# Reordering the first steps of a fused causal convolution and swish MLP: taps by DMA, bf16 blocks, output matmuls later

## The chip, the cores and the metric

The kernel runs on one core of a Trainium2 chip, in one launch. The metric is device time in microseconds (us). The core has a matrix engine (PE, or TensorE, with its weight loads PEld), a vector engine (DVE), a scalar engine (ACT, or ScalarE), GpSimd (POOL) and a sync engine (SP) that here only issues DMAs. POOL and ACT issue DMAs too. Each engine works through its own instructions in order and waits on semaphores for the others; DMAs run beside them all. Matmuls write to PSUM, from where DVE or ACT take the results to SBUF.

## The reference

Two things follow each other. The first is a causal depthwise convolution over the sequence with 7 taps; the taps are a softmax per head, 8 heads of 24 channels each. The second is an MLP with a swish whose slope `beta` differs per hidden channel.

```
x: (8, 4096, 192) f32;  weight: (8, 7);  w_in: (192, 2048);  w_out: (2048, 192);  beta: (2048,)
w   = softmax(weight, axis=-1)                      # 8 heads, 7 taps
y   = for each token: sum over k of w[head, k] * x[token - 6 + k]     (zeros before the sequence)
h   = y.reshape(32768, 192) @ w_in
g   = h * sigmoid(beta * h)
out = g @ w_out                                     # (32768, 192) f32
```

The kernel uses g*beta = silu(beta*h): ACT computes silu with `beta` as scale, and w_out is divided by beta beforehand.

## The kernel before, in words

**Streams and steps.** The 32768 tokens are two streams of 16384 (`NS = 2`) that go side by side. The 192 channels lie as three groups (`NK = 3`) of 64, so one stream fills 64 partitions and two fill 128. `steps` lists the chunks of each stream: step 0 and 1 of 128 tokens, step 2 to 8 of 256, the rest of 512. A tile is 512 tokens, a block 128, so steps 0 to 2 cover tile 0 with blocks 0, 1 and 2 to 3.

**What a step does.** For each of 16 groups of 128 hidden channels (`fc`) PE computes w_in times the convolved input into PSUM (`ph`, two buffers), and ACT takes it through silu into `g` (bf16, SBUF). In steps 0 to 2 `mm1_pair` (matmuls on line 315, ACT on line 319) does two groups at once, `u` and `u + 8`: the lower partitions use one half of w_in, the upper ones the other, so that w_in need be loaded only once by then. From step 3 on `mm1` (lines 332, 336) does one group for both streams, with the copies of w_in that `copy_w_in` (116) makes in the other partitions. The output matmuls of step i, `mm2` (366), read `g` and w_out_s and run during step i+1: `mm2_plan` spreads them over its units. They come in two phases, since PE works with 64 rows at a time on two banks; phase 1 ends with `store`, where DVE takes out the two banks (372) and SP stores them. In steps of 512 `mm2_quarters` (412) takes this place.

**The convolution.** From step 3 on DVE does it: 7 operations (296, 298) per step on transposed input `xt`, in the order of a work list that `vector_work` empties by a budget of DVE time. Tile 0 is convolved on PE instead: `transpose_0` (206) turns a block of `x0` with an identity matrix, `take_0` (211 on ACT, 213 on DVE) copies it to `xr[b]`, `halo_0` (217) copies its last 6 columns to the front of the next block's `xr`, `conv_0` (223) multiplies it by diagonal matrices `diag` of the taps, summing over the taps in PSUM, and `evac_0` (232, 234) scales by 1/sum and writes `xcp`. For tile 1, blocks 0 and 1 are transposed on PE too (540), the later ones by DMA transposes on SP (97) after a cast on DVE (86).

**The start.** The 8x7 taps are loaded by SP; a matmul with a selection matrix `sel` (made by POOL, 146) spreads them over 128 partitions (183); DVE takes the maximum (185), ACT the exponential (188). `warm` matmuls (178) on a tile of zeros keep PE busy before. POOL's queue then issues, in this order: w_in in pieces (113), blocks 2 and 3 of x (129) among them, w_out (157), tile 1 of x (80) and, after a wait, the copies of w_in. `scale_w_out` (268) divides w_out by beta on DVE, four groups at a time.

**Order.** Almost all instructions are pinned to program order, so each engine does them as the code lists them: in steps 0 and 1 the `if` chains in the main loop put transposes, convolution matmuls and scalings between the pairs of the first layer.

Of the kernel before, what the change touches and what calls it, by code (L numbers as in the profile page):

```python
# [19 lines left out]
def kernel(  # L20
# [17 lines left out]
    NK = 3  # L38
# [20 lines left out]
    g_pool = ctx.enter_context(tc.tile_pool(name="g", bufs=1))  # L59
# [59 lines left out]
    taps = consts.tile([H, K], FP32, name="taps")  # L119
    pin(nc.sync.dma_start(out=taps, in_=weight))  # L120
    x0 = consts.tile([128, NB, NS, D], FP32, name="x0")
    pin(nc.scalar.dma_start(out=x0[:, 0, 1, :], in_=xs[1, 0:128, :]))
    pin(nc.sync.dma_start(out=x0[:, 0, 0, :], in_=xs[0, 0:128, :]))
# [4 lines left out]
    def load_x0(b, eng):  # L128
        pin(eng.dma_start(out=x0[:, b, :, :],
                          in_=xs[:, 128 * b:128 * b + 128, :].rearrange("s p d -> p s d")))  # L130
# [3 lines left out]
    zeros = consts.tile([128, 256], BF16, name="zeros")  # L134
    pin(nc.vector.memset(zeros, 0.0))
# [5 lines left out]

    sel = consts.tile([H, NS, H, Q // H], FP32, name="sel")
    pin(nc.vector.memset(sel, 0.0))
    ident = consts.tile([128, 128], FP32, name="ident")
    pin(nc.vector.memset(ident, 0.0))
    pin(nc.gpsimd.affine_select(out=sel, in_=sel, compare_op=ALU.not_equal, fill=1.0, base=0,  # L146
                                pattern=[[0, NS], [-1, H], [0, Q // H]], channel_multiplier=1))
# [10 lines left out]
    for b in (0, 2):  # L158
        for s in range(NS):
            load_x(1, s, b, b + 2, nc.gpsimd)  # L160


    xr = [consts.tile([128, NK, PAD + 128], FP32R, name=f"xr{b}") for b in range(NB)]
    pin(nc.vector.memset(xr[0][:, :, 0:PAD].bitcast(FP32), 0.0))
# [8 lines left out]

    idle = psum_h.tile([128, 2, TILE], FP32, name="ph")

    def warm(n, cols):
        for _ in range(n):
            pin(nc.tensor.matmul(idle[:, 0, 0:cols], zeros[:, 0:128], zeros[:, 0:cols], start=True, stop=True))

    warm(8, 256)  # L180
    cv0 = psum_h.tile([128, 2, TILE], FP32, name="ph")
    tap_ps = cv0[:, 1, 0:K]
    pin(nc.tensor.matmul(tap_ps, sel.rearrange("h s g j -> h (s g j)"), taps, start=True, stop=True))
    nmax = consts.tile([128, 1], FP32, name="nmax")
    pin(nc.vector.tensor_reduce(out=nmax, in_=tap_ps, axis=AX.X, op=ALU.max, negate=True))
    etap = consts.tile([128, K], FP32, name="etap")
    tsum = consts.tile([128, 1], FP32, name="tsum")
    pin(nc.scalar.activation(etap, tap_ps, AF.Exp, bias=nmax, accum_out=tsum))
# [13 lines left out]
    def transpose_0(bank, b, src=x0):  # L202
        t = bank[:, 0:NK * 128].rearrange("p (k t) -> p k t", k=NK)
        v = src[:, b, :, :].rearrange("p s d -> p (s d)").rearrange("p (m k) -> p k m", k=NK)
        for kk in range(NK):
            pin(nc.tensor.transpose(t[:, kk, :], v[:, kk, :], ident))  # L206
        return t

    def take_0(t, b, act=False):
        if act:  # L210
            pin(nc.scalar.activation(xr[b][:, :, PAD:], t, AF.Copy))
        else:
            pin(nc.vector.tensor_copy(xr[b][:, :, PAD:], t))

    def halo_0(t, b):
        dst = xr[b + 1][:, :, 0:PAD] if b + 1 < NB else xt_of[0][:, :, TILE + LEAD - PAD:]
        pin(nc.vector.tensor_copy(dst, t[:, :, 128 - PAD:]))

    def conv_0(cv, b, k0=0, k1=K):

        for k in range(k0, k1):
            for s in range(NS):
                pin(nc.tensor.matmul(  # L223
                    cv[s][:, 0:NK * 128], diag[half_of(s), k, :, :].rearrange("p s q -> p (s q)"),
                    xr[b][half_of(s), :, k:k + 128], start=(k == 0), stop=(k == K - 1)))
# [12 lines left out]
    t = transpose_0(pa[0], 0)  # L238
    take_0(t, 0, act=True)
    warm(4, 128)  # L240
# [4 lines left out]
    halo_0(t, 0)  # L245
# [4 lines left out]
    pb = po_banks()  # L250
# [4 lines left out]
    beta_ps = idle[:, 1, 0:NF]  # L255
# [3 lines left out]
    t = transpose_0(pa[0], 1)  # L259
    take_0(t, 1)  # L260
    halo_0(t, 1)
# [46 lines left out]
    def mm1_pair(i, u):  # L308
# [9 lines left out]
        for h in range(2):  # L318
            pin(nc.scalar.activation(g_of[i][:, fcs[h], :, 0:n],  # L319
# [3 lines left out]
    def mm1(i, fc):  # L323
# [12 lines left out]
        pin(nc.scalar.activation(g_of[i][:, fc, :, 0:n], ph[:, :, 0:n], AF.Silu,  # L336
                                 scale=beta[:, fc:fc + 1]))

    def pairs_of(i):
        if steps[i][1] == 128:  # L340
            return [((0, 0), (1, 0))]
        return [((s, 0), (s, 1)) for s in range(NS)]

    def mm2_plan(i):
# [3 lines left out]
        if len(prs) == 1:  # L348
            order = [(prs[0], 0, 2 - 2 * i, 6), (prs[0], 1, 10, 16)]
        else:  # L350
            order = [(prs[p], ph, 8 * ph + 4 * p, 8 * ph + 4 * p + 4) for ph in range(2) for p in range(2)]
# [6 lines left out]
    def mm2(i, pr, phase, fc):  # L358
        if phase == 0 and fc == 0:
            po_of[pr] = po_banks()  # L360
        po = po_of[pr]
        for half in range(2):
# [3 lines left out]
            pin(nc.tensor.matmul(po[q][:, 0:D], g_of[i][r, fc, s, ts(b, 128)], w_out_s[r, fc, :],  # L366
# [33 lines left out]
    def mm2_quarters(count):  # L400
        for _ in range(count):
            turn = turns.pop(0)
            for s in range(NS):
                for r in range(2):
# [3 lines left out]
                    if (i, m) not in po_of:  # L408
# [4 lines left out]
                                         g_of[i][half_of(r), fc, s, 0:n],  # L413
# [28 lines left out]
    def last(i):  # L442
# [3 lines left out]
        for s in range(NS):  # L446
            for b in range(n // 128):
                po = po_bank()
                for fc in range(NF):
                    pin(nc.tensor.matmul(po[:, 0:D], g_of[i][:, fc, s, ts(b, 128)], w_out_s[:, fc, :],  # L450
# [35 lines left out]
    gs = [g_pool.tile([128, NF, NS, TILE], BF16, name=f"g{p}") for p in range(2)]  # L486
    for i in range(n_steps):
        plan = mm2_plan(i - 1) if 0 < i <= NQ else [[] for _ in range(NF)]
        g_of[i] = gs[i % 2]
        if i == 0:  # L490
            cv1, cv2, cv3 = pb, pa, pb
            for u in range(NF // 2):
                mm1_pair(0, u)
                if u == 0:
                    t = transpose_0(pb[0], 2)
                    take_0(t, 2)
                    halo_0(t, 2)
                elif u == 1:
# [96 lines left out]
```

## Time and profile before

| what | value |
|---|---|
| median of 9 runs | 692.16 us (691.69 to 694.86) |
| the profiled execution's own time | 691.73 us |
| its span, first to last instruction | 690.0 us |
| PE / ACT / DVE / POOL busy | 99% / 85% / 80% / 2% of the span |
| step 0 starts on PE (line 315) | 8.33 us |
| step 3 starts on PE (line 332) | 34.06 us |

The profile is one execution, taken by the hardware. Times count from the span's start. A group of instructions has its busy time and the idle time just before it, with what ended that idle time (the releaser). A busy PE is not PE at its peak, since matmuls are pipelined and their ends are modelled. Idle time on an engine that does not set the pace costs nothing.

### The profile page before, as it was taken

What the parts mean: (1) busy time and instruction counts of PE and PEld (TensorE: products, weight loads), DVE (VectorE), ACT (ScalarE), POOL (GpSimd) and SP (SyncE); (2) the same over time, 40 slices, a digit from 0 to 9 for tenths busy, and PEclk for the clock granted to TensorE, in tenths of its full rate; (3) what the DMA queues carried; (4) which work ended last, traced back from release to release, by engine and by line L of the source; (5) the groups of instructions that cost most, each with busy time, mean ns of one, the idle gap of its engine ahead of it and who ended that gap; (6) DMA issues with size and microseconds to landing.
All of it is one profiled execution on the core that took longest, in us unless ns stands there. A gap on an engine that the chain in (4) does not pass through costs nothing.

```text
span 690.0 us, 27516 instructions
## 1 busy us (share of the span) xinstructions
PE 683.5 (99%) x12425; PEld 429.7 (62%) x12425; DVE 553.8 (80%) x906; ACT 589.0 (85%) x600; POOL 14.5 (2%) x26
## 2 busy tenths in 40 slices
PE   8999999999999999999999999999999999999998
PEld 6699986555555555555555555555555555555557
DVE  5899899999998898878898888898888898876102
ACT  6899999888888888888888888888888888888881
POOL 8000000000000000000000000000000000000000
PEclk9999999999999999999999999999999999999999
DMA  9564333354434444234444233444234444220223
GB/s 221 154 126 116 113 106 87 83 123 116 104 79 105 109 117 115 68 69 106 110 117 114 53 85 106 110 117 115 51 87 105 111 116 71 53 47 22 48 48 93
DMA packets 148021, 67.26 MB, mean 97 GB/s; under 512 B 109520, under 2 KB 147104, under 8 KB 147904
## 3 DMA queue, kind: packets, MB, share of 16 engines
q1 hardware_dynamic: 145424, 61.08, 35.4%
q0 software_dynamic: 2336, 4.33, 2.7%
q8 instruction: 97, 1.59, 0.9%
q14 instruction: 20, 0.16, 0.1%
q10 hardware_dynamic: 144, 0.10, 0.1%
HBM read 28.32 MB, written 25.17 MB: 78 GB/s over the span
## 4 chain that ended last, share of the span: by engine, by line
PE 96%; ACT 2%; DMA 1%; POOL 0%; issue 0%; DVE 0%; POOLq 0%; ACTq 0%
PE ph L332 47%; PE po L412 41%; PE po L366 6%; ACT g L319 2%; PE po L450 2%; DMA x<-in_x_dram 1%; PE ph L315 1%; PE po L223 0%; POOL w_in_s L113 0%; PE po L206 0%; POOL sel L146 0%; DVE o_sp L372 0%; POOL ident L148 0%; POOLq L146 0%; POOLq L148 0%
## 5 line engine op out<-in xcount | busy, mean ns | idle before, releaser
L336 ACT ACTIVATE g<-ph,beta 128x1024 bf16<-128x1024 f32 (+1 forms) x544 | 562.4, 1039 | 78.2 <-PE ph L332 68.5
L332 PE MATMUL ph<-xc,w_in_s 64*64 64x512 bf16 (+2 forms) x5856 | 613.6, 366 | 0.3 <-ACT g L319 0.3
L412 PE MATMUL po<-g,w_out_q 64*64 64x512 bf16 x5184 | 552.7, 376 | 0.0
L332 PEld LDWEIGHTS <-w_in_s 64*64 64x64 bf16 (+1 forms) x5856 | 257.3, 104 | 152.8 <-issue 0.6
L298 DVE SCALAR_TENSOR_TENSOR acc<-xt,tapn,acc 128x512 f32<-128x512 bf16 (+1 forms) x450 | 311.4, 764 | 0.9
L412 PEld LDWEIGHTS <-w_out_q 64*64 64x64 bf16 x5184 | 242.1, 105 | 89.0
L429 DVE STREAM_TRANSPOSE o_sb<-po 128x512 f32<-128x512 f32 x81 | 71.9, 888 | 110.4 <-PE po L412 110.3
L366 PE MATMUL po<-w_out_s,g 64*128 64x192 bf16 x1024 | 65.0, 243 | 0.0
L298 DVE SCALAR_TENSOR_TENSOR xc<-xt,tapn,acc 128x512 bf16<-128x512 bf16 (+1 forms) x90 | 64.1, 765 | 0.2
L366 PEld LDWEIGHTS <-g 64*128 64x128 bf16 x1024 | 49.3, 94 | 5.5
L86 DVE CAST xb<-xf 128x768 bf16<-128x768 f32 (+1 forms) x62 | 48.5, 818 | 0.0
L296 DVE TENSOR_SCALAR acc<-xt,tapn 128x512 f32<-128x512 bf16 (+1 forms) x90 | 41.0, 488 | 1.1
L319 ACT ACTIVATE g<-ph,beta 128x256 bf16<-128x256 f32 (+1 forms) x48 | 22.3, 559 | 4.7 <-PE ph L315 4.5
L372 DVE COPY o_sp<-po 128x192 f32<-128x192 f32 x40 | 12.6, 350 | 10.3 <-PE po L450 4.4
L315 PE MATMUL ph<-xcp,w_in_s 64*128 64x256 bf16 (+1 forms) x144 | 14.7, 306 | 1.2 <-ACT g L319 1.1
L450 PEld LDWEIGHTS <-g 128*128 128x128 bf16 x128 | 10.5, 98 | 0.4 <-issue 0.4
L450 PE MATMUL po<-w_out_s,g 128*128 128x192 bf16 x128 | 10.7, 246 | 0.0
L315 PEld LDWEIGHTS <-w_in_s 64*128 64x128 bf16 x144 | 6.6, 94 | 5.0 <-issue 3.0
L234 DVE TENSOR_SCALAR xcp<-po,rsum 128x384 bf16<-128x384 f32 x7 | 4.0, 613 | 5.8 <-PE po L223 5.8
L223 PE MATMUL po<-xr,diag 64*128 64x384 f32 x49 | 8.4, 394 | 0.0
L223 PEld LDWEIGHTS po<-xr,diag 64*128 64x128 f32 x49 | 5.5, 206 | 0.2
L287 DVE COPY xt<-xt 128x18 bf16<-128x18 bf16 x28 | 4.2, 151 | 0.0
(50 smaller groups left out, 49.4 us busy)
## 6 DMA issues: line engine op xcount, KB each, us to landing
xf<-in_x_dram SPq DMA_DIRECT2D x60, 384.0 KB, 4.0
out_dram<-o_sb SPq DMA_DIRECT2D x108, 192.0 KB, 4.7
out_dram<-o_sp SPq DMA_DIRECT2D x16, 192.0 KB, 4.0
xt<-xb SPq DMA_TRANSPOSE x122, 3.0
w_out_f<-in_moe_w_out_dram POOLq DMA_DIRECT2D x4, 384.0 KB, 7.0
xf<-in_x_dram POOLq DMA_DIRECT2D x4, 192.0 KB, 7.8
w_in_s<-w_in_s POOLq DMA_DIRECT2D x4, 192.0 KB, 6.7
out_dram<-o_sp SPq DMA_DIRECT2D x8, 96.0 KB, 1.7
```

Source lines behind the costliest of these rows:

```text
L86: pin((eng or nc.vector).tensor_copy(xbf_of[j][:, b0:b1, :, s, :].rearrange("p b k q -> p k b q"), xf_of[j][:, b0:b1, s, :].rearrange("p b ...
L223: pin(nc.tensor.matmul(cv[s][:, 0:NK * 128], diag[half_of(s), k, :, :].rearrange("p s q -> p (s q)"), xr[b][half_of(s), :, k:k + 128], sta ...
L296: pin(nc.vector.tensor_scalar_mul(a, src, w))
L298: pin(nc.vector.scalar_tensor_tensor(out=xc_of[i][:, k0:k1, 0:n] if k == K - 1 else a, in0=src, scalar=w, in1=a, op0=ALU.mult, op1=ALU.add))
L315: pin(nc.tensor.matmul(ph[:, h, 0:NS * n], w_in_s[half_of(h), kk, ts(fcs[h], 128)], xc_of[i][half_of(h), :, kk, :], start=(kk == 0), stop= ...
L319: pin(nc.scalar.activation(g_of[i][:, fcs[h], :, 0:n], ph[:, h, 0:NS * n].rearrange("p (s t) -> p s t", s=NS), AF.Silu, scale=beta[:, fcs[ ...
L332: pin(nc.tensor.matmul(ph[m0:m1, s, 0:n], w_in_s[half_of(s), kk, 128 * fc + m0:128 * fc + m1], xc_of[i][half_of(s), kk, 0:n], start=(kk == ...
L336: pin(nc.scalar.activation(g_of[i][:, fc, :, 0:n], ph[:, :, 0:n], AF.Silu, scale=beta[:, fc:fc + 1]))
L366: pin(nc.tensor.matmul(po[q][:, 0:D], g_of[i][r, fc, s, ts(b, 128)], w_out_s[r, fc, :], start=(phase == 0 and fc == 0), stop=(phase == 1 a ...
L412: pin(nc.tensor.matmul(po_of[i, m][half_of(s), 0:n], w_out_q[half_of(r), fc, m, :], g_of[i][half_of(r), fc, s, 0:n], start=(first and fc = ...
L429: pin(nc.vector.transpose(osb_of[i][:, 0:n // L, :, m], po_of[i, m][:, 0:n].rearrange("p (b l) -> p b l", l=L)))
L450: pin(nc.tensor.matmul(po[:, 0:D], g_of[i][:, fc, s, ts(b, 128)], w_out_s[:, fc, :], start=(fc == 0), stop=(fc == NF - 1)))
```

## The change

- **Taps.** `sel`, its POOL instruction and the matmul go. `taps` is now 128 x 7, loaded by two DMAs (SP for the lower 64 partitions, ACT for the upper) whose source repeats each head's row 8 times. Block 0 of x is issued ahead of them on both queues.
- **Warm-up.** A constant tile of ones takes the place of zeros; 9 and 6 matmuls instead of 8 and 4.
- **Blocks 2, 3 of tile 0 and 0, 1 of tile 1** are loaded by POOL with a cast to bf16 (`xb0`, `xb1`) and transposed with a bf16 identity `ident_b`, made by one DVE copy.
- **Halos.** `xr` is one tile of 6 + 512 columns, so a block's halo lies in place. One copy at the end of step 1 gives tile 0's last 6 columns to DVE's convolution.
- **Order in steps 0 to 2.** `first_tile` lists transposes, convolutions and scalings anew: block 2's transposes come after pair 1 of step 0 instead of pair 0, block 3's convolution in pairs 0 to 2 of step 1 instead of 3 and 4, all scalings by pair 2 of step 1. `first_mm2` lists the output matmuls of chunks 0 and 1: chunk 0's first phase moves from pairs 1 and 2 of step 1 to its pairs 4 to 7, its second from pairs 5 to 7 of step 1 to pairs 3 and 4 of step 2; chunk 1's phases are at pairs 1 and 2 and at 5 to 7 of step 2.
- **g** is allocated per step and per half of the groups, with small buffers of their own for steps 0 and 1.

From step 3 on the order of work is the same. The core of the diff:

```diff
-    taps = consts.tile([H, K], FP32, name="taps")
-    pin(nc.sync.dma_start(out=taps, in_=weight))
-    x0 = consts.tile([128, NB, NS, D], FP32, name="x0")
-    pin(nc.scalar.dma_start(out=x0[:, 0, 1, :], in_=xs[1, 0:128, :]))
-    pin(nc.sync.dma_start(out=x0[:, 0, 0, :], in_=xs[0, 0:128, :]))
+    x0 = consts.tile([128, 2, NS, D], FP32, name="x0")
+    xb0 = consts.tile([128, 2, NS, D], BF16, name="xb0")
+    xb1 = consts.tile([128, 2, NS, D], BF16, name="xb1")
+    taps = consts.tile([128, K], FP32, name="taps")
+    for s, eng in enumerate((nc.sync, nc.scalar)):
+        pin(eng.dma_start(out=x0[:, 0, s, :], in_=xs[s, 0:128, :]))
+    for s, eng in enumerate((nc.sync, nc.scalar)):
+        pin(eng.dma_start(out=taps[half_of(s), :],
+                          in_=weight[:, None, :].to_broadcast([H, Q // H, K])))
...
-    for b in (0, 2):
-        for s in range(NS):
-            load_x(1, s, b, b + 2, nc.gpsimd)
-    xr = [consts.tile([128, NK, PAD + 128], FP32R, name=f"xr{b}") for b in range(NB)]
+    for s in range(NS):
+        pin(nc.gpsimd.dma_start(out=xb1[:, :, s, :],
+                                in_=xs[s, TILE:TILE + 256, :].rearrange("(b p) d -> p b d", p=128)))
+    for s in range(NS):
+        load_x(1, s, 2, NB, nc.gpsimd)
+    xr = consts.tile([128, NK, PAD + TILE], FP32R, name="xr")
...
-    warm(8, 256)
+    warm(9, 256)
...
-    tap_ps = cv0[:, 1, 0:K]
-    pin(nc.tensor.matmul(tap_ps, sel.rearrange("h s g j -> h (s g j)"), taps, start=True, stop=True))
-    pin(nc.vector.tensor_reduce(out=nmax, in_=tap_ps, axis=AX.X, op=ALU.max, negate=True))
+    pin(nc.vector.tensor_reduce(out=nmax, in_=taps, axis=AX.X, op=ALU.max, negate=True))
...
-            order = [(prs[0], 0, 2 - 2 * i, 6), (prs[0], 1, 10, 16)]
...
+    def new_g(i, half):
+        n, kind = (TILE, "g") if i > 1 else (128, "gp")
+        g_of[i, half] = g_pool.tile([128, NF // 2, NS, n], BF16, name=f"{kind}{half}")
+    def first_tile(i, u):
+        if (i, u) == (0, 1):
+            take_0(transpose_0(pa[0], xb0, 0), 2)
+            conv_0(pb, 1, 0, 1)
+        elif (i, u) == (0, 2):
+            take_0(transpose_0(pa[1], xb0, 1), 3)
+            conv_0(pb, 1, 1, 2)
+        elif (i, u) == (0, 3):
+            conv_0(pb, 1, 2, 5)
+        elif (i, u) == (0, 4):
+            conv_0(pb, 1, 5, K)
+            for s in range(NS):
+                evac_0(pb, 1, s, nc.vector)
+            for c in range(4):
+                scale_w_out(c)
...
+        elif (i, u) == (1, 2):
+            conv_0(pb, 3, 5, K)
+            for s in range(NS):
+                evac_0(pb, 3, s, nc.vector)
+            for c in range(8, NF):
+                scale_w_out(c)
+        elif (i, u) == (1, 6):
+            new_xt(1)
+            ts_ = [transpose_0(pb[b], xb1, b) for b in range(2)]
+            for b in range(2):
+                pin(nc.vector.tensor_copy(xt_of[1][:, :, LEAD + 128 * b:LEAD + 128 * b + 128], ts_[b]))
+            pin(nc.vector.tensor_copy(xt_of[0][:, :, TILE + LEAD - PAD:],
+                                      xr[:, :, TILE:].bitcast(FP32)))
...
+    for key, us, cuts in (((0, 0), [(1, 4), (1, 5), (1, 6), (1, 7)], (0, 4, 8, 12, 16)),
+                          ((1, 0), [(2, 1), (2, 2)], (0, 8, 16)),
+                          ((0, 1), [(2, 3), (2, 4)], (0, 8, 16)),
+                          ((1, 1), [(2, 5), (2, 6), (2, 7)], (0, 5, 10, 16))):
+        for (i, u), c0, c1 in zip(us, cuts, cuts[1:]):
+            first_mm2[(i, u) + key] = range(c0, c1)
...
     for i in range(n_steps):
         if i < NP:
             for u in range(NF // 2):
                 mm1_pair(i, u)
+                first_tile(i, u)
+                for ph in (0, 1):
+                    for j in range(i):
+                        for fc in first_mm2.get((i, u, j, ph), ()):
+                            mm2(j, prs_0, ph, fc)
```

## The prediction

> **What bounds the kernel now.** I read the page's busy shares first, then the same by stage, then ScalarE's order of work in the ramp, then the chain of waits. Columns of the stage view: stretch, its length, busy time of PE, PEld, DVE, ACT, POOL (instructions), granted clock, DMA share, GB/s.
>
> ```profile
> PE 683.5 (99%) x12425; PEld 429.7 (62%) x12425; DVE 553.8 (80%) x906; ACT 589.0 (85%) x600; POOL 14.5 (2%) x26
> ```
> ```profile
> 8.33:15.41 7.08, 6.34 (x76) 4.63 (x77) 4.46 (x14) 5.08 (x13) 5.77 (x9) 1.00 1.07 288
> 15.41:24.89 9.48, 9.03 (x141) 7.30 (x140) 6.43 (x20) 7.26 (x19) 1.43 (x3) 1.00 0.65 166
> 24.89:34.06 9.17, 8.51 (x117) 5.25 (x113) 8.92 (x14) 8.89 (x17) 0.00 (x0) 1.00 0.60 169
> 34.06:98.90 64.84, 64.52 (x1348) 63.62 (x1347) 61.02 (x96) 64.70 (x98) 0.00 (x0) 1.00 0.47 119
> 98.90:676.29 577.39, 577.39 (x10593) 333.15 (x10590) 466.06 (x738) 498.66 (x449) 0.00 (x0) 1.00 0.36 89
> ```
> The rows are steps 0, 1, 2, then 3 to 8, then all steps of 512 tokens. From step 3 on TensorE never stands still, and the change leaves that part's work and order as they are. So the time is the start of step 3 (34.06 us) plus a constant, and a microsecond won before it is one at the end. In steps 0 to 2 PE looks busy too, but ScalarE decides there: its time in the swish is fixed, so its idle time is what can be won.
>
> ```profile
> 8.87 0.84 ACT L319 ACTIVATE g<-ph,beta 128x256 bf16<-128x256 f32 x2 [0.76 <-PE ph L315]
> 10.67 0.84 ACT L319 ACTIVATE g<-ph,beta 128x256 bf16<-128x256 f32 x2 [0.95 <-PE ph L315]
> 11.93 7.32 ACT L319 ACTIVATE g<-ph,beta 128x256 bf16<-128x256 f32 x18 [0.42 <-PE ph L315]
> 20.17 0.84 ACT L319 ACTIVATE g<-ph,beta 128x256 bf16<-128x256 f32 x2 [0.93 <-PE ph L315]
> 21.24 2.55 ACT L319 ACTIVATE g<-ph,beta 128x256 bf16<-128x256 f32 x6 [0.23 <-PE ph L315]
> 24.68 0.84 ACT L319 ACTIVATE g<-ph,beta 128x256 bf16<-128x256 f32 x2 [0.90 <-PE ph L315]
> 25.80 9.36 ACT L319 ACTIVATE g<-ph,beta 128x512 bf16<-128x512 f32 x16 [0.28 <-PE ph L315]
> ```
> Columns: start, duration, instruction, count, and the idle time before it with its releaser. Between the first swish (8.87) and step 3's first (34.98) the idle times add up to 3.7 us: 1.4 in step 0, 1.2 in the middle of step 1, 1.2 around its end. The chain of waits names what PE was late for.
>
> ```profile
> 1.22 0.40 POOL sel L146
> 1.62 0.25 POOL ident L148
> 1.87 2.57 POOL w_in_s L113 x4
> 4.44 5.09 DMA x<-in_x_dram
> 9.57 0.62 PE po L206 x3
> ...
> 18.37 1.44 PE po L366 x16
> ...
> 22.91 0.89 PE po L206 x6
> 23.79 0.52 PE po L366 x10
> ```
> In step 0, PE stood before the transposes of block 2, whose load was issued from the POOL queue at 4.44 and landed at 9.53; the second weight matmuls stood behind. In step 1, sixteen output matmuls, worth 0.66 us, took 1.44: they read w_out_s, which DVE is still scaling (twelve L268 from 16.66 to 19.49). Near 23 us, six fp32 transposes and ten output matmuls lie between two pairs of the first layer.
>
> **The change, part by part.**
>
> Start. The tap matmul, sel (a DVE memset of 0.17 and 0.40 us on POOL) and the zeros memset (0.17) go. POOL then reaches its first w_in load near 1.4 instead of 1.87, and everything in its queue (w_in, blocks 2 and 3, w_out, tile 1, w_in copies) is issued 0.45 us earlier. SP keeps four loads: block 0 moves to 0.74, taps to 1.15, beta and block 1 stay. ACT issues one load more (0.39 us) ahead of its table load, which ends at 2.8 instead of 2.44: covered, since the exponential waits for taps. Block 0 took 1.9 us to land, beta 1.7; taps as 64 rows of 28 B on each queue has no row. Bounds: 1.7, and 3.1 (block 1's 192 KB). I take 2.0, as it follows a 96 KB load: about 3.15, the maximum 0.2 us later, the exponential near 3.5, against 3.71. Block 0's copy follows it. The convolution of block 0 starts near 4.5 (4.89 before), and the first swish near 8.5 (8.87). With taps at 3.1 us all this is 0.7 later, most of which the next wait covers.
>
> Step 0. PE now issues two pairs of the first layer before the transposes of block 2, so what counts is when xb0 lands. Issued near 4.0. Nearest rows: cast loads from the same queue, 3.8 us (96 KB of w_in) and 4.8 (144 KB); the uncast block 2, 5.1 (192 KB); the worst x load there, 7.8 (tile 1, behind w_out). xb0 reads 192 KB and writes 96 KB in 256 rows, so I take 5.3: landed 9.3. Ends: 3.8, where ScalarE's own pace decides, and 7.8, landed 11.8. Then three bf16 transposes at 0.1 us each (a 128x128 bf16 weight load took 98 ns; fp32 ones took 0.18), one pair of convolution matmuls 0.16, and the next first-layer pair 0.54 until its swish starts (8.33 to 8.87): the third pair's swish at 10.3, against 11.93 before.
>
> The Trainium skill's "DMA: Bandwidth & Descriptors" (Specifications) speaks against the cast: below 512 B per run the engine reads, modifies and writes, and xb0 writes runs of 384 B. If that doubled a load's 0.9 us of engine time (an estimate from the spacing of the w_in landings), the third swish would come 0.9 us later and the sum be 1.8 instead of 2.7; no run here shows it.
>
> Steps 0 and 1. From the third pair on ScalarE goes at 0.407 us each (18 in 7.32), 0.81 a pair. PE's load per pair: 0.33 for the first layer plus at most three convolution pairs, 0.5. That is 0.83, level with ScalarE. The scaling of w_out_s (16 of 0.236 us on DVE) keeps its length, but the output matmuls of chunk 0 start at pair 4 of step 1 instead of pair 1, after DVE has finished, so the stalled 0.8 us and most of the 1.2 us idle go. The halo copies (0.15 to 0.17 us on DVE) were in nobody's way; one 18-column copy remains, 0.1 us. At pair 6 the transposes cost 0.6 instead of 0.9 and four output pairs 0.33 with 0.33 for the layer: 1.26 against 0.81, less what the two ph buffers cover; I leave 0.2 us idle, and 0.2 for block 3's landing.
>
> Step 2. Three phases of 16 output pairs come here instead of two: 48 x 0.082 = 3.9 us, plus 8 x 0.65 for the first layer: 9.1, under ScalarE's 9.36. But pairs 1 to 4 hold 8 output pairs each: 0.65 + 0.66 = 1.31 against 1.17. Four times 0.14, and the 0.28 at its start, less cover by the buffers: 0.7 idle.
>
> Behind it: DVE's chain to step 3's xc. Before it ran from 23.49 to 33.05, 1.0 us ahead of need. Chunk 0's two take-outs (0.61) move from ahead of the taps to just before the last tap, where they wait for PE at pair 4 of step 2 (near 28.7 us, while the sixth tap ends near 29.1). The chain starts with the transposes, hence shifts with them; it stays about 0.8 ahead. What waits behind it: the casts and SP's transposes and loads, which move with it. Tile 1's casts need loads landed by 21.5; those took 7.8 us from an issue at 13.1 at the latest. g's separate halves let ScalarE wait, once per half, on matmuls long finished: nothing.
>
> Sum. 10.3 + 14 x 0.81 + 9.36 + (0.2 + 0.2 + 0.7) = 32.3 for step 3's first swish, against 34.98: 2.7 us won. The profiled execution took 691.73 us (span 690.0): 689.0. The median of the nine is 0.43 above it: 692.16 - 2.7 = 689.4.
>
> TensorE's clock: the rows show a granted 1.00 throughout, yet the seven convolution pairs of block 0 came 0.32 us apart (4.89 to 7.5) and those after 11.6 us 0.16 to 0.17 apart: half rate at first. The Trainium skill's "TensorE: Matmul & The Clock Gate" (Part 1) says that a busy window of about 3.4 us, free-running, opens it. By the rule the longer warm-up (nine and six instead of eight and four, from 0.8 us) may open it by 4.5, and 1.1 us would go from block 0's convolution. My sum has nothing of it, since xb0 lands at 9.3 either way.
>
> **The rivals.**
> (a) The cast loads land late, at 7.8 us like tile 1's. For: DMA is full between 8 and 15 us (share 1.07). Against: w_in's cast loads took 3.8 and 4.8. Third swish at 12.8: 0.2 us won, 691.9, no change.
> (b) Slower: a cast load costs the DMA engines 3 us more than a plain one, at that same full stage. Block 2 lands 3 us and block 3 6 us late, w_in's last piece behind them; the fourth pair's swish starts near 17 instead of 11.1. That loses 5.9 against the forecast, 3.2 net of the 2.7: 694.9. It decides from about 1.5 us per load. Against it: the first four w_in casts landed about 1 us apart.
> (c) The idle time goes only halfway: taps land at the late end, step 2 is PE's (1.31 for all eight pairs, 10.5 us), and ScalarE waits 1.1 us more: 1.4 us won, 690.8.
> (d) The deferral does not do what it says: output matmuls still meet unscaled w_out_s, because w_out's loads land late, and 1.2 us stays: 1.5 won, 690.7.
>
> **How the numbers follow.** Forecast 0.56, (c) 0.12, (d) 0.10, (a) 0.12, (b) 0.10. A measurement of this kernel tells no less than about 0.2% (1.4 us) from no change. (c) and (d) lie near this bound and on its faster side, so faster 0.78, same 0.12 from (a), slower 0.10 from (b). Low end: no idle but 0.4 us and a first swish at 8.3 give 31.1, 3.9 won: 688.3, and 0.4 for the spread of runs: 687.9. High end: (a) and a little: 692.0.
>
> **What would show it.** Right: first w_in load near 1.4; block 2's transposes shorter and after two first-layer groups, starting near 9.3; ScalarE idle under 1.5 us between first swish and step 3; no output matmuls in the first four pairs of step 1; step 3 near 31.4. Wrong: a DMA release of those transposes past 11 us; idle ScalarE inside step 2 of over 1 us; DVE's last tap of step 3's xc releasing PE; convolution of block 0 still at half rate after 8 us.

## The result: 0.5% faster by the medians, where 0.4% was forecast

The changed kernel took 688.65 us in the median of 11 runs (687.19 to 689.32), the kernel before 692.25 in 34 (691.45 to 694.86). The medians give a ratio of 0.9948; taken over all runs, as the ratios below are too, it is 0.9938, 95% interval 0.9928 to 0.9947. The profiled execution of the changed kernel took 687.37 us, of before 691.73: 4.36 us between the two that are compared now. The medians lie 3.6 us apart, the forecast had 2.7.

The busy shares on the page after hardly differ from those before; ScalarE is at 86 instead of 85%.

```profile
PE 679.5 (99%) x12426; PEld 450.9 (66%) x12426; DVE 552.9 (81%) x902; ACT 586.4 (86%) x600; POOL 14.2 (2%) x25
```

The view by stage tells more. It is cut as the one before was: at the first layer's first matmul of steps 0, 1, 2, 3 and 9, and at the last step's output matmuls.

```profile
8.43:14.72 6.29, 6.29 (x83) 4.63 (x83) 3.93 (x12) 5.58 (x15) 4.81 (x7) 1.00 1.10 295
14.72:21.11 6.39, 6.16 (x102) 5.05 (x102) 5.96 (x20) 6.02 (x17) 1.86 (x3) 1.00 0.88 215
21.11:30.54 9.43, 9.43 (x149) 6.65 (x146) 9.22 (x14) 9.20 (x17) 0.00 (x0) 1.00 0.64 183
30.54:94.38 63.84, 63.52 (x1348) 63.18 (x1345) 60.67 (x96) 63.52 (x98) 0.00 (x0) 1.00 0.43 118
94.38:671.90 577.52, 577.52 (x10598) 356.67 (x10592) 466.30 (x738) 497.75 (x449) 0.00 (x0) 1.00 0.35 89
```

The second number of each row, the stage's length, set against before:

| stage | before | after | difference |
|---|---|---|---|
| up to step 0 | 8.33 | 8.43 | +0.10 |
| step 0 | 7.08 | 6.29 | -0.79 |
| step 1 | 9.48 | 6.39 | -3.09 |
| step 2 | 9.17 | 9.43 | +0.26 |
| steps 3 to 8 | 64.84 | 63.84 | -1.00 |
| steps of 512, up to the last output | 577.39 | 577.52 | +0.13 |

Two things stand out. The start, which had lost a matmul, a POOL instruction and two memsets, came no earlier. And a whole microsecond went in steps 3 to 8, where the order of work is the same.

ScalarE's order of work in the ramp shows where the idle time went (start, duration, instruction, count, idle time before it and its releaser):

```profile
5.15 0.30 ACT L189 ACTIVATE etap<-taps,nmax 128x7 f32<-128x7 f32 x1 [1.24 <-DVE nmax L186]
...
8.97 11.67 ACT L317 ACTIVATE gp<-ph,beta 128x256 bf16<-128x256 f32 x30 [0.76 <-DVE xr L217]
20.99 0.84 ACT L317 ACTIVATE gp<-ph,beta 128x256 bf16<-128x256 f32 x2 [0.35 <-PE ph L313]
21.97 9.67 ACT L317 ACTIVATE g<-ph,beta 128x512 bf16<-128x512 f32 x16
31.50 29.14 ACT L334 ACTIVATE g<-ph,beta 128x512 bf16<-128x512 f32 x44
```

Fifteen pairs follow each other in one row; of the 3.7 us of idle time that the view lists before, between first swish and step 3, it lists 0.35 now. The first swish came at 8.97 instead of 8.87, step 3's first at 31.50 instead of 34.98. So the ramp gave 3.48 us in this execution, and steps 3 to 9 another 1.12: 0.82 from step 3's first swish to step 9's (64.65 to 63.83) and 0.30 within step 9 (16.73 to 16.43). What follows gave 0.23 back.

Why the start was no earlier is read from ScalarE's exponential of the taps before, which came at 3.71, and from the chain of waits after:

```profile
3.71 0.27 ACT L188 ACTIVATE etap<-ph,nmax 128x7 f32<-128x7 f32 x1 [1.06 <-DVE nmax L185]
```
```profile
0.74 0.38 SPq L124
1.13 0.06 issue
1.18 3.67 DMA taps<-in_weight_dram
4.90 0.05 issue
4.95 0.17 DVE nmax L186
5.15 0.39 ACT etap L189 x2
5.54 0.39 ACT xr L215
```

The taps, spread by DMA, took 3.67 us from issue until DVE could use them. Before, their eight rows took 1.36 us, from the issue at 0.74 to the last count on their semaphore at 2.10. And the convolution that waited for them then ran at nearly twice the rate it had before (PE's order of work, before and after):

```profile
5.38 0.52 PE L223 MATMUL ph<-xr,diag 64*128 64x384 f32 x1
5.38 0.52 PE L223 MATMUL po<-xr,diag 64*128 64x384 f32 x1
5.70 0.52 PE L223 MATMUL ph<-xr,diag 64*128 64x384 f32 x1
5.70 0.52 PE L223 MATMUL po<-xr,diag 64*128 64x384 f32 x1
```
```profile
6.46 0.34 PE L223 MATMUL ph<-xr,diag 64*128 64x384 f32 x1
6.47 0.34 PE L223 MATMUL po<-xr,diag 64*128 64x384 f32 x1
6.64 0.33 PE L223 MATMUL ph<-xr,diag 64*128 64x384 f32 x1
6.65 0.34 PE L223 MATMUL po<-xr,diag 64*128 64x384 f32 x1
...
9.19 0.35 PE L209 MATMUL po<-ident_b,xb 128*128 128x128 bf16 x3
```

Pairs 0.18 us apart, against 0.32 before. The last line answers the step that the forecast turned on: block 2's transposes came at 9.19, right behind the first layer's matmuls, and waited for no DMA.

The theory to test was then: the ramp's gain is the later output matmuls and the new order around them; the new g tiles are the gain after step 3; the taps' DMA is a loss, made up in this execution by TensorE's clock, which is chance.

### The profile page after: what moved, and what is told of

It is laid out like the page before. It is cut to its first block, busy times and chain, and to the rows that moved or that the text cites. A ratio compares the mean times of both kernels' runs of the same rounds, so it can differ in the third digit from the quotient of the medians.

```text
span 685.6 us, 27039 instructions
## 1 busy us (share of the span) xinstructions
PE 679.5 (99%) x12426; PEld 450.9 (66%) x12426; DVE 552.9 (81%) x902; ACT 586.4 (86%) x600; POOL 14.2 (2%) x25
## 4 chain that ended last, share of the span: by engine, by line
PE 97%; ACT 1%; DMA 1%; issue 0%; DVE 0%; SPq 0%; DVEq 0%
PE ph L330 47%; PE po L408 41%; PE po L362 6%; PE po L446 2%; PE ph L313 1%; ACT gp L317 1%; DMA taps<-in_weight_dram 1%; ACT g L317 1%; PE po L209 0%; PE ph L223 0%; PE po L223 0%; ACT etap L189 0%; ACT xr L215 0%; SPq L124 0%; DVE o_sp L368 0%
## 5 line engine op out<-in xcount | busy, mean ns | idle before, releaser
L330 PE MATMUL ph<-xc,w_in_s 64*64 64x512 bf16 (+2 forms) x5856 | 589.5, 366 | 0.3 <-ACT g L317 0.3
L408 PE MATMUL po<-g,w_out_q 64*64 64x512 bf16 x5184 | 528.5, 376 | 0.0
L330 PEld LDWEIGHTS <-w_in_s 64*64 64x64 bf16 (+1 forms) x5856 | 272.1, 104 | 126.2 <-issue 0.5
L362 PE MATMUL po<-w_out_s,g 64*128 64x192 bf16 x896 | 57.0, 243 | 0.0
L362 PEld LDWEIGHTS <-g 64*128 64x128 bf16 x896 | 43.4, 94 | 3.3
L317 ACT ACTIVATE gp<-ph,beta 128x256 bf16<-128x256 f32 x32 | 12.3, 480 | 1.3 <-DVE xr L217 0.8
L446 PEld LDWEIGHTS <-g 128*128 128x128 bf16 x128 | 10.5, 98 | 0.4 <-issue 0.4
L317 ACT ACTIVATE g<-ph,beta 128x512 bf16<-128x512 f32 x16 | 9.6, 691 | 0.2
L362 PE MATMUL po<-w_out_s,gp 64*128 64x192 bf16 x128 | 7.2, 243 | 0.0
L362 PEld LDWEIGHTS <-gp 64*128 64x128 bf16 x128 | 5.8, 94 | 1.6
```

The lines of the kernel that those rows point to most:

```text
L317: pin(nc.scalar.activation(g_at(i, fcs[h])[:, :, 0:n], ph[:, h, 0:NS * n].rearrange("p (s t) -> p s t", s=NS), AF.Silu, scale=beta[:, fcs[ ...
L330: pin(nc.tensor.matmul(ph[m0:m1, s, 0:n], w_in_s[half_of(s), kk, 128 * fc + m0:128 * fc + m1], xc_of[i][half_of(s), kk, 0:n], start=(kk == ...
L362: pin(nc.tensor.matmul(po[q][:, 0:D], g_at(i, fc)[r, s, ts(b, 128)], w_out_s[r, fc, :], start=(phase == 0 and fc == 0), stop=(phase == 1 a ...
L408: pin(nc.tensor.matmul(po_of[i, m][half_of(s), 0:n], w_out_q[half_of(r), fc, m, :], g_at(i, fc)[half_of(r), s, 0:n], start=(first and fc = ...
L446: pin(nc.tensor.matmul(po[:, 0:D], g_at(i, fc)[:, s, ts(b, 128)], w_out_s[:, fc, :], start=(fc == 0), stop=(fc == NF - 1)))
```

## Experiments

All ran beside the kernel before on the same chip, and ratios are to it. Its median was 691.99; beside the later output matmuls alone and beside taps' DMA ahead of block 0 it was 693.35, since 10 of its 17 runs there lie above 693. So where a difference of tenths of a microsecond matters, the lengths of stages in the profiles are used, one execution for each kernel.

### g in kept tiles again

```diff
+    kept = {(p, h): consts.tile([128, NF // 2, NS, TILE], BF16, name=f"g{h}{p}")
+            for p in range(2) for h in range(2)}
+
     def new_g(i, half):
-        n, kind = (TILE, "g") if i > 1 else (128, "gp")
-        g_of[i, half] = g_pool.tile([128, NF // 2, NS, n], BF16, name=f"{kind}{half}")
+        if i > 1:
+            g_of[i, half] = kept[i % 2, half]
+        else:
+            g_of[i, half] = g_pool.tile([128, NF // 2, NS, 128], BF16, name=f"gp{half}")
```

> The changed kernel with one part undone: g of steps 2 and on lies again in tiles that are kept for the whole program (two sets of two halves), so each swish again waits for ScalarE's own earlier write to the same place. Theory (the new g tiles take these waits away and are worth the part of the gain that appears after step 3): steps 3 to 8 take 10.7 us each again instead of 10.57, step 9 0.3 us more; the time rises from 688.65 by 0.8 to 1.2 us, to about 689.6. Rival (that part comes from the ramp, or from the state of the clock): steps 3 to 8 stay at 10.57 and the time at 688.65.

690.08 us (689.54 to 692.52, 12 runs), ratio 0.9975 (0.9965 to 0.9984). From step 3's first swish to step 9's 64.76 us, with the new tiles 63.83; step 9 16.73 against 16.43. That is 1.23 us in the place where the theory had it. The view of ScalarE's line in steps 3 to 8 shows the mechanism: EVENT_SEMAPHORE counts waits that its queue carries out as instructions of their own, ahead of a swish. First the kernel before, then after, then this one:

```profile
L336 ACT ACTIVATE g<-ph,beta x96: 687/687/763, 35.0 to 98.7; 128x512 bf16<-128x512 f32 x96
L336 ACTq EVENT_SEMAPHORE  x81: 17/17/17, 35.8 to 98.6; - x81
```
```profile
L334 ACT ACTIVATE g<-ph,beta x96: 687/687/721, 31.5 to 94.3; 128x512 bf16<-128x512 f32 x96
L334 ACTq EVENT_SEMAPHORE  x10: 17/17/17, 42.1 to 89.7; - x10
```
```profile
L334 ACT ACTIVATE g<-ph,beta x96: 679/687/721, 32.4 to 96.2; 128x512 bf16<-128x512 f32 x96
L334 ACTq EVENT_SEMAPHORE  x73: 17/17/17, 43.0 to 96.2; - x73
```

In a kept tile almost every swish overwrites what ScalarE itself wrote two steps earlier, and the trace has it wait on ScalarE's own semaphore beside PE's: 82 of the 96 swishes before and 73 here, against 10 after. The instruction takes as long as otherwise, but such a swish starts 0.10 us after the last of its matmuls ends instead of 0.04. It frees its `ph` buffer that much later, and PE needs the same buffer again two groups on. With kept tiles PE starts a group 0.05 us (median) after the swish that frees its buffer ends, after the change 0.08, so there it mostly no longer waits for it. PE's order of work before and after, the first layer's groups alone:

```profile
46.52 0.51 PE L332 MATMUL ph<-xc,w_in_s 64*128 64x256 bf16 x6
...
47.20 0.50 PE L332 MATMUL ph<-xc,w_in_s 64*128 64x256 bf16 x6
...
47.86 0.50 PE L332 MATMUL ph<-xc,w_in_s 64*128 64x256 bf16 x6
```
```profile
44.86 0.51 PE L330 MATMUL ph<-xc,w_in_s 64*128 64x256 bf16 x6
...
45.52 0.51 PE L330 MATMUL ph<-xc,w_in_s 64*128 64x256 bf16 x6
...
46.18 0.51 PE L330 MATMUL ph<-xc,w_in_s 64*128 64x256 bf16 x6
```

Every second group comes 0.68 us after the last instead of 0.66. Two groups take 1.340 us in the median of steps 4 to 8, before and with g kept, and 1.315 after: 0.01 us per swish.

### The kernel before with new g tiles alone

```diff
-    g_pool = ctx.enter_context(tc.tile_pool(name="g", bufs=1))
+    g_pool = ctx.enter_context(tc.tile_pool(name="g", bufs=2))
...
-    gs = [g_pool.tile([128, NF, NS, TILE], BF16, name=f"g{p}") for p in range(2)]
+    def new_g(i, half):
+        g_of[i, half] = g_pool.tile([128, NF // 2, NS, TILE], BF16, name=f"g{half}")
...
```

> The kernel before with that part alone: g allocated per step and per half of the groups. Theory: ramp as before (step 3's first swish near 35.0), steps 3 to 8 at 10.57 us each, so 0.8 to 1.2 us won: about 691.2 against 692.25. Rival: no difference, 692.25.

691.11 us (690.46 to 692.5, 11 runs), ratio 0.9988 (0.9979 to 0.9997): 0.88 us less in the medians. Steps 3 to 8 took 63.92 instead of 64.65 from swish to swish, step 9 16.43 instead of 16.73: 1.03 us. The waits are gone here too:

```profile
L336 ACTq EVENT_SEMAPHORE  x11: 17/17/17, 40.7 to 93.5; - x11
```

The part works alone as it does with the others.

### The later output matmuls alone, on the kernel before

```diff
+    first_mm2 = {}
...
-                    pt = po_banks()
+                    pt = pb
-                for t in plan[2 * u] + plan[2 * u + 1]:
-                    mm2(i - 1, *t)
+                for ph in (0, 1):
+                    for j in range(i):
+                        for fc in first_mm2.get((i, u, j, ph), ()):
+                            mm2(j, prs_0, ph, fc)
```

(`first_mm2` is filled as in the change; the edit of g's tiles is not shown again.)

> The kernel before with two parts of the change alone: g in new tiles per step and half, and the output matmuls of chunks 0 and 1 at their new, later places (the transposes of tile 1 use the banks of block 3 again, so that banks suffice). Taps by matmul, fp32 blocks, halo copies and the places of convolution and scaling as before. Theory (the later output matmuls alone take away ScalarE's idle time of 0.9 us in the middle of step 1 and most of that around its end, and g is worth 1.1): step 1 takes about 7.2 us instead of 9.1, step 3's first swish near 33 instead of 35, the time 692.0 less 3: about 689.0. Rival (the ramp's gain needs the bf16 transposes and the new places too): step 1 stays above 8 us and the time above 690.2.

690.08 us (689.64 to 692.37, 12 runs), ratio 0.9965 (0.9955 to 0.9975). The profiles put the first swish of the steps, and the time that each step took from there, thus:

| from first swish to first swish | before | before + later output matmuls + g | after |
|---|---|---|---|
| step 0 | 7.83 | 7.54 | 6.33 |
| step 1 | 9.10 | 7.76 | 6.67 |
| step 2 | 9.18 | 9.53 | 9.53 |

Neither side had it quite. The later output matmuls take 1.34 us out of step 1 and put 0.35 into step 2. The stall on w_out_s is gone, but two of the waits stay, as ScalarE's order of work in this kernel shows:

```profile
10.48 0.84 ACT L319 ACTIVATE gp<-ph,beta 128x256 bf16<-128x256 f32 x2 [0.68 <-PE ph L315]
11.75 7.81 ACT L319 ACTIVATE gp<-ph,beta 128x256 bf16<-128x256 f32 x20 [0.42 <-PE ph L315]
...
20.97 1.57 ACT L319 ACTIVATE gp<-ph,beta 128x256 bf16<-128x256 f32 x4 [0.38 <-PE ph L315]
23.29 0.84 ACT L319 ACTIVATE gp<-ph,beta 128x256 bf16<-128x256 f32 x2 [0.75 <-PE ph L315]
```

The first two are step 0's, where PE still waits 0.47 us for block 2 and transposes it in fp32; the last stands behind the six fp32 transposes of tile 1. The rest of the change, the bf16 blocks and the new order, takes another 1.2 us from step 0 and 1.1 from step 1. Which of the two does it was not taken apart in full; in step 1 it is not the cast of blocks 2 and 3 of tile 0, as the run of that cast shows below.

### Output matmuls early again, in the changed kernel

```diff
-    for key, us, cuts in (((0, 0), [(1, 4), (1, 5), (1, 6), (1, 7)], (0, 4, 8, 12, 16)),
-                          ((1, 0), [(2, 1), (2, 2)], (0, 8, 16)),
-                          ((0, 1), [(2, 3), (2, 4)], (0, 8, 16)),
-                          ((1, 1), [(2, 5), (2, 6), (2, 7)], (0, 5, 10, 16))):
+    for key, us, cuts in (((0, 0), [(1, 1), (1, 2)], (0, 8, 16)),
+                          ((0, 1), [(1, 5), (1, 6), (1, 7)], (0, 6, 11, 16)),
+                          ((1, 0), [(2, 0), (2, 1), (2, 2)], (0, 6, 11, 16)),
+                          ((1, 1), [(2, 5), (2, 6), (2, 7)], (0, 6, 11, 16))):
```

> The changed kernel with the output matmuls of chunks 0 and 1 at about their old places (chunk 0 in pairs 1, 2 and 5 to 7 of step 1; chunk 1 in pairs 0 to 2 and 5 to 7 of step 2), all else as changed. Theory (the deferral takes away ScalarE's idle time in steps 1 and 2): PE meets unscaled w_out_s in step 1 again, ScalarE's idle time between first swish and step 3 rises from 0.6 to about 2 us or more, the time by 1.5 to 2 us, to about 690.4. Rival (bf16 blocks and the new places of convolution and scaling took the idle time away): less than 0.5 us more, under 689.2.

692.88 us (692.21 to 694.47, 12 runs), ratio 1.0011 (1.0000 to 1.0022): slower than expected by more than 2 us, and no faster than the kernel before. Step 1 took 10.94 us. PE's order of work:

```profile
18.16 0.62 PE L223 MATMUL po<-xr,diag 64*128 64x384 f32 x4
20.22 1.86 PE L362 MATMUL po<-w_out_s,gp 64*128 64x192 bf16 x16 [1.44 <-DVE w_out_s L266]
```

The change moved the last eight scalings of w_out_s behind block 3's convolution. Output matmuls at their old place then wait not only for the scaling but for the convolution and its two evictions ahead of it on DVE: 1.44 us of idle PE, and sixteen matmuls in 1.86. So the two moves belong together. What this run prices is early output matmuls in the new order; it does not price the deferral, which the run before does.

### Blocks 2 and 3 in fp32

```diff
-    xb0 = consts.tile([128, 2, NS, D], BF16, name="xb0")
+    xb0 = consts.tile([128, 2, NS, D], FP32, name="xb0")
```

> The changed kernel with blocks 2 and 3 of tile 0 loaded and transposed in fp32 again (blocks 0 and 1 of tile 1 stay bf16). Theory (the cast halves the bytes to write, hence lands 1 us earlier than the fp32 load, and the transposes are 0.3 us shorter each): block 2 lands at about 9.1 instead of 8.1, PE waits for it shortly, the third pair's swish comes 0.3 to 0.6 us later: about 689.1. Rival (the cast makes no difference, since PE comes to the transposes only at 9.2 us): 688.65 within 0.2.

689.07 us (687.81 to 689.57, 5 runs), ratio 0.9954 (0.9943 to 0.9966). Its interval overlaps the changed kernel's, and the profiled execution can't settle the time: taps came later in it (exponential at 5.71), and PE fell back to half rate after the convolution, so that it reached the transposes only at 10.62, when block 2 had landed (9.13; the cast one had landed at 8.42 in the changed kernel). The lengths of its steps say a little more. From swish to swish step 0 took 7.40 us, against 7.10 in another execution of the changed kernel in which half rate ended about as late (12.1 us, the next run; 11.57 here); step 1 took 6.67, the same as with the cast. So these two casts are worth nothing in step 1 and perhaps 0.3 us in step 0, from one execution of each.

### The changed kernel again, and its clock

> The changed kernel unaltered, on the same chip as the three that follow. Theory (executions fall into two groups, 687.3 and 688.7 us, by whether TensorE's half rate ends before or after the convolution of block 0, which starts near 6 us): if the profiled execution is near 688.7, its convolution pairs come 0.32 us apart and the first swish near 9.9; if it is near 687.3, 0.17 us apart and 9.0. Rival (the groups come from the landing of taps or from something later): the spacing of the pairs does not go with the time.

689.49 us (688.12 to 691.33, 6 runs), ratio 0.9964 (0.9949 to 0.9978). The same kernel, and an interval that lies beside the first one's; its six runs do not fall into two groups either. The profiled execution took 689.41 us, 2.04 more than the first. PE's order of work has the difference:

```profile
6.56 0.52 PE L223 MATMUL ph<-xr,diag 64*128 64x384 f32 x1
...
6.88 0.52 PE L223 MATMUL ph<-xr,diag 64*128 64x384 f32 x1
...
9.38 1.46 PE L313 MATMUL ph<-xcp,w_in_s 64*128 64x256 bf16 x12
10.78 0.50 PE L209 MATMUL po<-ident_b,xb 128*128 128x128 bf16 x3
```

Pairs 0.32 us apart, and the first layer's first twelve matmuls in 1.46 instead of 0.83. The first swish came at 10.24 and step 3's at 33.54, and from there on all is as in the first execution (63.83, 16.43). The trace's record of the clock has full rate from 4.4 us on in the first execution and from 12.1 in this one. With g kept it was 9.2, first swish 9.90. So these executions differ by what TensorE's clock does in the first 12 us: 1.27 us until the first swish and 0.77 in step 0 make up the 2.04. What the runs at 690.86 and 691.33 lost beyond that was not profiled. Page and stage rows, which give a granted clock of 1.00 throughout, don't show it; the distance between matmuls does.

### More and fewer warm-up matmuls

```diff
-    warm(6, 128)
+    warm(16, 128)
```

> The changed kernel with 16 instead of 6 warm-up matmuls before the convolution of block 0, which fill most of the 1.3 us in which TensorE waits there for taps. Theory (TensorE's idle time before the convolution lets the half rate last longer in most executions): the pairs come 0.17 us apart in more of the executions, median near 687.5 instead of 688.65. Rival (the moment at which full rate comes is chance, whatever stands before): 688.65, the same two groups.

687.48 us (687.12 to 687.91, 5 runs), ratio 0.9932 (0.9920 to 0.9944), apart from the unaltered kernel's beside it, though not from that of the first result. None of the five is above 687.91, where 3 of the unaltered kernel's 17 were below it. In the profiled execution PE works until 5.88 and goes to full rate at 7.1, in the middle of the convolution; the first swish is at 9.49.

```profile
6.71 0.51 PE L223 MATMUL ph<-xr,diag 64*128 64x384 f32 x1
...
7.03 0.37 PE L223 MATMUL ph<-xr,diag 64*128 64x384 f32 x1
...
7.24 0.33 PE L223 MATMUL ph<-xr,diag 64*128 64x384 f32 x1
```

```diff
-    warm(9, 256)
+    warm(1, 128)
...
-    warm(6, 128)
```

> The changed kernel with one small warm-up matmul instead of nine and six. Theory (the earlier warm-up is what brings the full rate before block 0's convolution in part of the executions): it comes after the convolution in all, and part of step 0 too goes at half rate: 689.2 to 690.5. Rival (no effect of the warm-up): 688.65.

688.99 us (688.53 to 691.2, 9 runs), ratio 0.9960 (0.9947 to 0.9974). None is under 688.53, where the changed kernel had three of eleven at 687.4 and less. But the unaltered kernel beside it had 689.49, and the intervals overlap, so the time alone does not tell this run from it. In the profiled execution the whole convolution goes at half rate, as expected, and the first swish is at 10.34.

The Trainium skill's "TensorE: Matmul & The Clock Gate" (Part 1) has full rate after a busy window of some 3.4 us whose phase is free. These runs agree in kind: the moment differs between executions of one kernel (4.4 and 12.1 us), was 7.1 in the execution with PE kept busy, and did not come before the end of the convolution in the one without warm-up. The length shows too. With blocks 2 and 3 in fp32 the record of the clock has full rate from 4.75 to 8.16 us, half from there to 11.57, and full again: 3.41 us each. In that execution PE had stood idle from 4.81 to 6.57, waiting for taps. Which idle time brings the half rate back was not tested.

### Taps spread by a matmul

```diff
-    taps = consts.tile([128, K], FP32, name="taps")
-    for s, eng in enumerate((nc.sync, nc.scalar)):
+    taps8 = consts.tile([H, K], FP32, name="taps8")
+    pin(nc.sync.dma_start(out=taps8, in_=weight))
+    for s, eng in ((1, nc.scalar), (0, nc.sync)):
         pin(eng.dma_start(out=x0[:, 0, s, :], in_=xs[s, 0:128, :]))
-    for s, eng in enumerate((nc.sync, nc.scalar)):
-        pin(eng.dma_start(out=taps[half_of(s), :],
-                          in_=weight[:, None, :].to_broadcast([H, Q // H, K])))
...
+    sel = consts.tile([H, NS, H, Q // H], FP32, name="sel")
+    for s in range(NS):
+        pin(nc.vector.tensor_copy(sel[:, s, :, :], ident[0:H, 0:H, None].to_broadcast([H, H, Q // H])))
...
+    taps = cv0[:, 1, 0:K]
+    pin(nc.tensor.matmul(taps, sel.rearrange("h s g j -> h (s g j)"), taps8, start=True, stop=True))
```

> The changed kernel with the taps spread by a matmul again: 8 rows of 28 B loaded first on SP, the selection matrix copied by DVE from the identity matrix (nothing of it on POOL), all else as changed. Theory (spread by DMA, taps land at 4.9 us where they took 1.6 us before, and hold up the convolution of block 0 by more than a microsecond): the maximum is taken near 3.5 instead of 4.95, the convolution starts near 4.7 instead of 6.0, the first swish near 8.0 at full rate or 8.6 at half rate; the third pair's swish is bound by block 2's landing at 8.1 and comes near 9.3 to 9.7 instead of 10.5. Time 0.8 to 1.2 us less, about 687.6, and the two groups closer together. Rival (the wait for taps is covered, since the convolution only changes from full to half rate when it starts earlier): 688.65.

687.66 us (686.99 to 687.92, 5 runs), ratio 0.9933 (0.9921 to 0.9944), again apart from the unaltered kernel's beside it. ScalarE's order of work:

```profile
3.62 0.27 ACT L192 ACTIVATE etap<-ph,nmax 128x7 f32<-128x7 f32 x1 [0.96 <-DVE nmax L189]
...
9.13 3.27 ACT L320 ACTIVATE gp<-ph,beta 128x256 bf16<-128x256 f32 x8 [1.10 <-PE ph L316]
```

The exponential is 1.5 us earlier than in the changed kernel. The convolution started at 4.81 and went at half rate throughout, yet the first swish came at 9.13: 0.8 and 1.1 us before those with taps by DMA at half rate (9.90 with g kept, 10.24 unaltered), and behind the execution with the early clock (8.97) by 0.16. The third pair's swish, 10.57, was not as early as expected, since at half rate the first one wasn't; but the load of block 2 did not hold it up.

### Taps' DMA ahead of block 0

```diff
     for s, eng in enumerate((nc.sync, nc.scalar)):
-        pin(eng.dma_start(out=x0[:, 0, s, :], in_=xs[s, 0:128, :]))
-    for s, eng in enumerate((nc.sync, nc.scalar)):
         pin(eng.dma_start(out=taps[half_of(s), :],
                           in_=weight[:, None, :].to_broadcast([H, Q // H, K])))
+    for s, eng in enumerate((nc.sync, nc.scalar)):
+        pin(eng.dma_start(out=x0[:, 0, s, :], in_=xs[s, 0:128, :]))
```

> The changed kernel with the two loads of taps issued ahead of block 0 of x on SP and ACT, all else as changed. Theory (the spread of 64 rows of 28 B is slow in itself: 0.8 and 1.2 us to issue and 3.7 us to land, where 8 such rows took 0.4 and 1.6): taps land at about 4.0 to 4.4 in place of 4.9, block 0 about 1 us later than 3.2, and the convolution starts near 5.4 instead of 6.0; the time changes by less than 0.6 us. Rival (taps were late because they stood behind block 0's 256 rows): taps land by 3.0, the convolution starts by 5.0 behind block 0, and 0.8 us or more is won.

689.18 us (689.04 to 690.21, 5 runs), ratio 0.9950 (0.9938 to 0.9963). The maximum was taken at 4.19, so taps need until then even when nothing is ahead of them: the spread is slow in itself, as the theory had it. But what it holds up was underrated. ACT's and PE's order of work:

```profile
0.74 1.21 ACTq L124 DMA_DIRECT2D taps<-in_weight_dram  x1
1.98 0.35 ACTq L127 DMA_DIRECT2D x<-in_x_dram  x1
```
```profile
5.65 0.88 PE L209 MATMUL po<-ident,x 128*128 128x128 f32 x3 [2.79 <-DMA x<-in_x_dram]
```

Block 0 is issued 1.2 us later on ACT and usable 2.4 us later than in the changed kernel (3.27), and PE idles 2.79 us. The convolution began at 7.11, not near 5.4. With taps by a matmul it began at 4.81, with their DMA behind block 0 at 5.78 to 6.01: the two DMAs of 1.8 KB cost its start about a microsecond or more wherever they stand. The time itself does not tell this run from the changed kernel.

## Why the prediction was right, and where it was not

**What bounds it**: right in the main. In all twelve profiled executions what follows step 9 takes 573.6 to 573.9 us, so the time follows from the start of step 3 and the pace of steps 3 to 9. But that pace was taken for fixed, on the reading that TensorE never stands still from step 3 on. In steps 3 to 8 it waited a little for ScalarE, 0.025 us in two groups, and ScalarE's own waits had a part in the pace.

**Start**: the taps were mis-sized. The prediction took 2.0 us from issue to landing, within 1.7 and 3.1; it was 3.67, outside both bounds. The kernel before had a row of them, 1.36 us, but for 8 rows of 28 B; after there are 128 on two queues, whose issue alone took 0.79 and 1.19 us (SP's and ACT's, where 0.41 and 0.39 had been seen). The first swish, forecast at 8.5, came at 8.97 in the execution with an early clock and at 9.9 and 10.2 in others. The prediction let the wait for block 2 cover late taps, and a gain from the clock too; as that load came early, it covered neither, and both count in full. That the clock came early in the profiled execution, at 4.4 where the prediction said 4.5 was possible, is luck: of the five profiled executions with this start, two had full rate before 5 us and three only after 9. In the unaltered kernel's second profile the convolution was still at half rate at 8 us, which the prediction had named as a sign of being wrong; its time, 689.41, was in the range all the same. POOL's 0.45 us came as forecast (1.42 for 1.87).

**Step 0**: the size was right for other reasons. The third pair's swish was forecast at 10.3 and came at 10.41. But xb0, put at 5.3 us, landed 4.4 us after its issue, at 8.42, and bound nothing; first swish and PE's pace did. The rule of the Trainium skill's "DMA: Bandwidth & Descriptors" (Specifications) on runs under 512 B, weighed against the change, did not show as a cost: in the trace the packets of 384 B of xb0 and xb1 took 51 ns in the median, those of 512 and 768 B of w_in 60 and 79, so the shorter ones lie on the same line as the longer.

**Steps 0 and 1**: the pace was better than 0.81 us a pair, 0.78 (30 swishes in 11.67), which over 14 pairs is 0.5 us; the stall on w_out_s went as forecast, and in the run that puts the output matmuls back it came again. The idle time of 0.2 at the transposes of tile 1 became 0.35.

**Step 2**: forecast 9.36 plus 0.7 idle, measured 9.53 from swish to swish. The two `ph` buffers covered more than was allowed for.

**DVE's chain**: right. The last tap of step 3's xc ended at 29.19, 1.35 us ahead of its use (0.8 forecast), with the take-outs at 27.65 waiting for nothing that counted.

**g**: this is the step that failed. "Matmuls long finished: nothing" looked at what the new waits add, and not at the waits of ScalarE on itself that the old tiles had. They were worth 1.23 us after step 3, seen by putting the kept tiles back, and 1.03 by taking the new tiles alone to the kernel before.

**The sum**: its terms add up to 32.1 us, not to the 32.3 that stands there, so 2.9 us and not 2.7 was what they forecast for the ramp. (b)'s 694.9 is counted from the profiled execution's time; from the median it is 695.4. Compared at half rate, with the run that keeps g (step 3's first swish at 32.43, the ramp as in the changed kernel), the ramp gave 34.98 - 32.43 = 2.55; with the early clock 3.48. Adding some 1.1 for g gives 3.65 and 4.6, less 0.2 given back at the end; the medians differ by 3.6. So the total was low by the term costed at nothing. Inside the ramp the late taps nearly cancelled against the faster pace and a cheaper step 2, and that they did so is luck.

**The rivals**: (a) and (b) are out, the cast loads landed early. (c) is half true: the taps came beyond their late end, and PE was busy throughout step 2 (9.43 of 9.43 us), but the step took 9.53 us and not 10.5. (d) is out: no output matmul of the changed kernel waited for w_out_s.

**Better versions**: more warm-up (687.48) and taps by matmul (687.66) both beat the kernel before and the unaltered changed kernel (689.49), which ran beside them. The two together were not tried.

## What to carry to other kernels

Writing again into a tile that is kept for the whole program can cost each instruction a wait on its own engine; allocating the buffer anew per use left 10 of 82 such waits here. Where an engine is close to the pace, count them in the trace before costing a change of tiles at nothing. A small load is priced by its rows and its issue, not by its bytes: 3.6 KB in 128 rows took 3.67 us, 224 B in 8 rows 1.36, and the difference was more than the matmul that it replaced had cost. And a change in the first ten microseconds is compared at the same state of TensorE's clock, read from the distance between matmuls, or the difference between two executions is taken for that of two kernels.

## What the runs showed that was not expected

- Two executions of one kernel differ by 2 us through TensorE's clock alone: full rate from 4.4 us in one, from 12.1 in the other. Ten more small matmuls where PE would idle made five runs agree within 0.8 us.
- A wait of ScalarE on its own earlier write makes a swish start 0.06 us later after its matmuls. Through the two buffers of `ph` about 0.01 us per swish of that reached the time (1.0 to 1.2 us over steps 3 to 9), without showing as listed idle time or as a longer instruction.
- Two DMAs of 64 rows of 28 B took 0.79 us (SP) and 1.19 us (ACT) to issue, against 0.36 to 0.42 for loads of 96 and 192 KB.
